# The last bank of the MLP in column halves, and three one-column products on ScalarE

## The chip, the cores and the metric

The kernel runs on one core of one Trainium2 chip. The metric is device time in microseconds (us) of one execution, as a median of several. PE is TensorE, PEld its weight loads, DVE is VectorE, ACT is ScalarE, POOL is GpSimd and SP is SyncE, which here does nothing but issue DMAs in order. L699 means line 699 of the kernel. Lines are given for the kernel before; from line 1415 on the changed kernel's lines stand 3 higher.

## What is computed

Two layers over a sequence of 2048 rows of 512 columns, each a linear attention block and a gated MLP, both added to the row they read:

```python
def _A_ref(x, wqkv, wo):            # H = 32 heads of 16
    q, k, v = ...                   # x @ wqkv, split by head
    phi = lambda t: jnp.where(t > 0, t + 1, jnp.exp(t)) + 1e-6
    pq, pk = phi(q), phi(k)
    kv = jnp.einsum("bhsd,bhse->bhde", pk, v)
    z = jnp.einsum("bhsd->bhd", pk)
    num = jnp.einsum("bhqd,bhde->bhqe", pq, kv)
    den = jnp.einsum("bhqd,bhd->bhq", pq, z)[..., None] + 1e-6
    ...
    return heads_joined(num / den) @ wo

def _B_ref(x, w1, w3, w2):          # w1, w3: 512x1792, w2: 1792x512
    return (_silu(x @ w1) * (x @ w3)) @ w2

x = A_x
x = x + _A_ref(_layernorm(x), A_wqkv, A_wo)
x = x + _B_ref(_layernorm(x), B_w1, B_w3, B_w2)
x = x + _A_ref(_layernorm(x), A_wqkv, A_wo)
x = x + _B_ref(_layernorm(x), B_w1, B_w3, B_w2)
```

## The kernel before

Rows live in SBUF as 16 tiles of 128 rows in fp32 (`x_sb`). Every matrix is scaled by a power of two and split into a high and a low fp16 part, and every product is made of three fp16 passes (`PASSES`). The scale factors are columns of 128x1 in one small tile, `scalars`: each factor is made once and used through the program. Among them are `co` (what the attention's output is multiplied by as it is added to a row, L667 and L668) and `cb` (the same for the MLP's output, L698 to L700). `co` is a product of two factors and `cb` of three; the three multiplications, L668, L699 and L700, are each a 128x1 tensor_tensor on DVE.

In layer 0 the weights of the MLP are prepared while the attention runs: `prepare_w2` (L695) makes the scale of w2 and then `cb`; `w13_group` (L544) takes sums and differences of blocks of w1 and w3 on POOL (L568 to L574) and splits them into high and low parts, the high part on ACT (L440), the low part, `split_late`, on DVE (L442). The order of the instructions on each engine is fixed by the order in which the program issues them: `in_order` pins it in this stage, and tables (FILLS, HOOKS, TURN and others) say where each piece of preparation stands between the pieces of the attention and the MLP. A scheduler places what is not pinned.

The end of layer 0's attention overlaps the start of its MLP. The last row tiles go through `weigh_in`, `weigh_out` (the queries' features, L881 and L1191, the denominator, L1193 to L1212, the low part on POOL, L1220, and a transposing DMA), `attn_out` (matmuls into a bank po) and `attn_add` (L1235 on DVE adds to the row, L1239 and L1240 on ACT take mean and squares). At the same time `mlp_rows` normalises the rows of the next 512 on ACT (L495), makes sums of column blocks (L1263 to L1266, 128x256 each, DVE for half of them) and copies to fp16 on ACT (L1270) and POOL or DVE (L1276).

The MLP works on chunks c of 512 rows and groups g of hidden columns, with seven products of 2x2 blocks in place of eight (`mlp_group`, L1311: matmuls at L518 into the banks ba, bb and bc, copied out by ACT at L1334 and added up by DVE at L1337). The 7 groups are taken in two sets per layer (`SETS`), each over all 4 chunks: 8 passes a layer. The multiplication by w2 goes into banks po, for the first and the second half (`sub`) of each row tile pair. A pass marked "plain" uses `mlp_out_plain` (L1390) with two banks of 128x512, one for each of two row tiles; the last pass of layer 1 is such a pass. Each bank's two column halves are filled by matmuls of their own, 128x256 (L1401).

At the very end (L1593 to L1604) the last group's matmuls are issued bank by bank (`by_bank`), for `sub` 0 and then for `sub` 1: 12 matmuls for the first bank, then 12 for the second. Then `mlp_add` (L1413) adds each bank to its rows in one 128x512 DVE instruction (L1417) and, for `sub` 1, where `engine is None`, stores each row tile by a DMA of 256 KB (`store_row`, L1410) right behind its add. The kernel ends when the last of these stores has landed.

Of the kernel before, what the change touches and what calls it, by code (L numbers as in the profile page):

```python
# [11 lines left out]
AF = mybir.ActivationFunctionType  # L12
OP = mybir.AluOpType
# [5 lines left out]
S, D, F, H = 2048, 512, 1792, 32  # L19
# [69 lines left out]
def kernel(  # L89
# [10 lines left out]
    nc = tc.nc  # L100
    x_rows = x_in.rearrange("b (t p) d -> p (b t) d", p=P)
    out_rows = out.rearrange("b (t p) d -> p (b t) d", p=P)
# [228 lines left out]
    x_sb = view(AT_X, F32, NT, D)  # L331
# [320 lines left out]
    def prepare_vo():  # L652
        yield AT["v"]
        yield from attn_bound("v", 2)
        yield AT["o"]
        yield from attn_bound("o", 3)
        pair_ = [weight_scale(n, info[n], 2.0**14) for n in "vo"]
        for a, _ in zip(*pair_):
            yield a
        for n, i, dst in (("v", 2, wv_s), ("o", 3, wo_s)):  # L660
            for k in range(NK):
                split_late(dst[:, 0, k, :], dst[:, 1, k, :], st_att[i][:, k, :], info[n][2])
                yield heavy[0]
        settle()
        nc.sync.dma_start(att_d["v"], wv_s)
        nc.sync.dma_start(att_d["o"], wo_s)
        co = scaled(info["v"][1], 2.0**-15)  # L667
        nc.vector.tensor_tensor(co, co, info["o"][1], OP.mult)  # L668
        info["co"] = co
        for _ in range(4):  # L670
            w2_load()
# [23 lines left out]
    def prepare_w2():  # L695
        yield has("w2_bound")
        yield from weight_scale("w2", bounds["w2"], 2.0**12)
        cb = scaled(info["w1"][1], 2.0**-5)  # L698
        nc.vector.tensor_tensor(cb, cb, info["w3"][1], OP.mult)  # L699
        nc.vector.tensor_tensor(cb, cb, info["w2"][1], OP.mult)  # L700
        info["cb"] = cb

    AT = {
# [686 lines left out]
    def mlp_out_plain(sub, g, hs, acc, ends, by_bank=False):  # L1390

        cs = slice(sub * P, (sub + 1) * P)
        w2 = w2_s[g]
        order = [(a, bs, n) for a, bs in ((0, (0, 1)), (1, (0,))) for n in range(2)]
        if by_bank:
            order.sort(key=lambda part: part[2])
        for a, bs, n in order:
            for i, qx in enumerate(((0, 3), (2, 1))[n]):
                for b in bs:
                    for half in range(2):  # L1400
                        nc.tensor.matmul(  # L1401
                            acc[n][:, half * HALF : (half + 1) * HALF],
                            hs[:, a, qx, cs],
                            w2_a21[g][:, b] if (i, half) == (0, 1) else w2[:, b, i + half],
                            start=g == ends[0] and i + a + b + half == 0,
                            stop=g == ends[1] and i == 1 and a == 1 and half == 1,
                            skip_group_check=True,
                        )

    def store_row(t):  # L1410
        nc.sync.dma_start(out_rows[:, t, :], x_sb[:, t, :])

    def mlp_add(sub, c, acc, engine):  # L1413

        if len(acc) == 2:
            for t, po in zip((4 * c + sub, 4 * c + 2 + sub), acc):
                nc.vector.scalar_tensor_tensor(  # L1417
                    x_sb[:, t, :], po, info["cb"], x_sb[:, t, :], OP.mult, OP.add
                )
                if engine is None:  # L1420
                    store_row(t)
            return
        a0, a1, a2, a3 = acc
        cb = info["cb"]
        u = view(AT_UV if engine is not None else late_at, F32, 3, HALF)
        x0 = x_sb[:, 4 * c + sub, :].rearrange("p (h n) -> p h n", h=2)
        x1 = x_sb[:, 4 * c + 2 + sub, :].rearrange("p (h n) -> p h n", h=2)

        def add(dst, src, to):
            nc.vector.scalar_tensor_tensor(dst, src, cb, to, OP.mult, OP.add)  # L1430

        nc.scalar.activation(u[:, 0], a0[:, :HALF], AF.Copy, scale=cb)
        if engine is None:

            add(u[:, 1], a0[:, HALF:], u[:, 0])
            add(u[:, 2], a1[:, :HALF], u[:, 1])
            add(x1[:, 0], a1[:, HALF:], x1[:, 0])
            nc.vector.tensor_tensor(x1, x1, u[:, 1:], OP.add)
            nc.vector.tensor_tensor(x0, x0, u[:, 0::2], OP.add)
            add(x0, a2.rearrange("p (h n) -> p h n", h=2), x0)  # L1440
            store_row(4 * c + sub)
            add(x1, a3[:, None, :HALF].to_broadcast([P, 2, HALF]), x1)
            store_row(4 * c + 2 + sub)
            return
        add(x0, a2.rearrange("p (h n) -> p h n", h=2), x0)
        add(x1, a3[:, None, :HALF].to_broadcast([P, 2, HALF]), x1)
        add(x1[:, 0], a1[:, HALF:], x1[:, 0])
        add(u[:, 1], a0[:, HALF:], u[:, 0])
        add(u[:, 2], a1[:, :HALF], u[:, 1])
        engine.tensor_tensor(x0, x0, u[:, 0::2], OP.add)  # L1450
        engine.tensor_tensor(x1, x1, u[:, 1:], OP.add)
# [292 lines left out]
```

## Time and profile before

| | |
|---|---|
| three runs | 1180.77, 1183.33, 1184.78 us; median 1183.33 us |
| the profiled execution | 1182.41 us, with a span of 1180.7 us from first to last instruction |
| PE busy | 1148.0 us, 97% of the span |
| DVE, ACT, POOL busy | 70%, 54%, 36% |
| granted TensorE clock, mean | 0.999 of full speed |

The profile is that of one execution. An instruction's busy time is read with its count; a busy PE is not PE at its peak. "idle before <-X" behind a row is the time in which its engine had nothing to do, and the work that ended it.

### The profile page before, as it was taken

To read this page: it belongs to the slowest core of one execution; us is meant where nothing else is said; L and a number is where in the kernel's file an instruction comes from. 1 tells how busy PE (TensorE), PEld (TensorE's weight loads), DVE (VectorE), ACT (ScalarE), POOL (GpSimd) and SP (SyncE) were. 2 spreads that over 40 slices of the span, in tenths; PEclk is the share of its full clock that TensorE was granted. 3 is DMA by queue.
4 is the path that set the end of the run, shared out by engine and by line. 5 is a ranking of instruction groups with operands and counts; after the bars stand their busy time and mean duration, and the time that the engine had idled before them with its cause. 6 is when DMAs were issued, how large, how long until landed. Compare 5 with 4: busy or idle time off the path is not lost.

```text
span 1180.7 us, 21818 instructions
## 1 busy us (share of the span) xinstructions
PE 1148.0 (97%) x8868; PEld 863.3 (73%) x8868; DVE 831.0 (70%) x1383; ACT 638.8 (54%) x1078; POOL 420.6 (36%) x488
## 2 busy tenths in 40 slices
PE   8999998899999999999999999999999999999998
PEld 3444444788888888888864454467888888888887
DVE  6778898977877886767774559756855775756543
ACT  5777687856544454434456644775544344443422
POOL 5342589402000144235268714684542210102010
PEclk9999999999999999999999999999999999999999
DMA  8977575979542221111416434664351350121000
GB/s 258 342 207 245 113 171 110 270 246 294 159 143 99 81 81 64 63 64 64 81 53 180 103 110 105 130 156 112 99 139 64 126 188 26 57 79 37 1 37 37
DMA packets 163396, 147.43 MB, mean 125 GB/s; under 512 B 129632, under 2 KB 138976, under 8 KB 158688
## 3 DMA queue, kind: packets, MB, share of 16 engines
q1 hardware_dynamic: 163296, 146.04, 42.7%
q8 instruction: 69, 1.13, 0.4%
q14 instruction: 31, 0.25, 0.1%
HBM read 72.48 MB, written 42.07 MB: 97 GB/s over the span
## 4 chain that ended last, share of the span: by engine, by line
PE 60%; DVE 15%; ACT 7%; POOL 6%; DMA 6%; issue 3%; SPq 1%; POOLq 0%; ACTq 0%; DVEq 0%
PE bb L518 16%; PE po L1381 13%; PE bc L518 8%; PE gt L518 5%; PE pk L518 5%; PE ba L518 4%; PE po L518 3%; PE pq L518 3%; DMA arena<-arena 3%; DMA arena<-in_B_w_dram 3%; PE po L1401 2%; DVE arena L1290 2%; DVE arena L1337 2%; DVE arena L442 2%; DVE arena L1430 2%
## 5 line engine op out<-in xcount | busy, mean ns | idle before, releaser
L518 PEld LDWEIGHTS <-arena 128*128 128x128 f16 x6360 | 618.3, 98 | 257.0 <-issue 16.1
L518 PE MATMUL bb<-arena 128*128 128x256 f16 x2688 | 329.5, 273 | 6.6 <-ACT arena L1334 4.0
L1381 PE MATMUL po<-arena 128*128 128x256 f16 x1932 | 234.6, 273 | 9.0 <-ACT arena L1293 6.4
L1381 PEld LDWEIGHTS <-arena 128*128 128x128 f16 x1932 | 187.8, 98 | 35.5 <-ACT arena L1293 9.3
L1295 DVE TENSOR_TENSOR arena<-arena 128x512 f16<-128x512 f32 (+1 forms) x104 | 114.5, 1100 | 105.5 <-ACT arena L1293 105.2
L1334 ACT ACTIVATE arena<-bb 128x512 f32<-128x512 f32 x196 | 114.8, 589 | 122.8 <-PE bb L518 82.1
L518 PE MATMUL bc<-arena 128*128 128x256 f16 x1344 | 165.8, 273 | 0.7 <-ACT arena L1334 0.5
L1293 ACT ACTIVATE arena<-arena 128x512 f16<-128x512 f32 x112 | 99.8, 891 | 120.4 <-DVE arena L1308 46.9
L1289 ACT ACTIVATE arena<-arena,scalars 128x512 f32<-128x512 f32 x112 | 74.7, 667 | 116.0 <-DVE arena L1337 115.5
L1290 DVE SCALAR_TENSOR_TENSOR arena<-arena,scalars 128x512 f32<-128x512 f32 x112 | 88.5, 790 | 51.7 <-ACT arena L1289 51.6
L1337 DVE TENSOR_TENSOR arena<-arena,bc 128x512 f32<-128x512 f32 x112 | 76.5, 683 | 55.0 <-ACT arena L1334 44.4
L1450 POOL TENSOR_TENSOR arena<-arena 128x512 f32<-128x512 f32 x25 | 35.2, 1409 | 207.6 <-DVE arena L1430 207.6
L1430 DVE SCALAR_TENSOR_TENSOR arena<-po,scalars,arena 128x256 f32<-128x256 f32 (+1 forms) x170 | 92.1, 585 | 9.1 <-PE po L1381 7.6
L518 PE MATMUL pk<-arena 128*128 128x512 f16 x384 | 89.8, 384 | 2.2 <-DMA arena<-arena 2.1
L518 PE MATMUL po<-arena 128*128 128x512 f16 x384 | 87.8, 379 | 3.2 <-DMA arena<-arena 2.1
L518 PE MATMUL gt<-arena 128*128 128x512 f16 x384 | 87.8, 379 | 0.6 <-ACT arena L946 0.4
L518 PE MATMUL pq<-arena 128*128 128x512 f16 x384 | 87.6, 379 | 0.1
L518 PE MATMUL ba<-arena 128*128 128x256 f16 x672 | 87.1, 273 | 0.0
L1305 POOL TENSOR_TENSOR arena<-arena 128x256 f32<-128x256 f32 x15 | 11.9, 792 | 148.7 <-DVE arena L1290 148.7
L495 ACT ACTIVATE arena<-arena,nb_all,rs_all 128x512 f32<-128x512 f32 x64 | 50.5, 807 | 26.5 <-POOL nb_all L492 26.3
L1401 PE MATMUL po<-arena 128*128 128x256 f16 x480 | 56.8, 273 | 0.4 <-ACT arena L1293 0.4
L1276 POOL TENSOR_TENSOR arena<-arena 128x512 f16<-128x512 f32 (+2 forms) x33 | 47.4, 1460 | 26.0 <-DMA arena<-arena 19.8
(163 smaller groups left out, 1289.4 us busy)
## 6 DMA issues: line engine op xcount, KB each, us to landing
arena<-xb_d SPq DMA_DIRECT2D x12, 1792.0 KB, 7.1
xb_d<-arena SPq DMA_DIRECT2D x8, 1792.0 KB, 5.9
xt_d<-arena SPq DMA_DIRECT2D x32, 256.0 KB, 2.9
arena<-xt_d SPq DMA_DIRECT2D x32, 256.0 KB, 3.3
arena<-in_B_w_dram SPq DMA_DIRECT2D x8, 896.0 KB, 6.7
arena<-in_B_w_dram SPq DMA_DIRECT2D x28, 256.0 KB, 3.4
w_d<-arena SPq DMA_DIRECT2D x4, 1792.0 KB, 10.8
arena<-w_d SPq DMA_DIRECT2D x4, 1792.0 KB, 6.7
```

The lines of the kernel that those rows point to most:

```text
L495: nc.scalar.activation(dst, x_sb[:, t, :], AF.Identity, scale=rs_all[:, t : t + 1], bias=nb_all[:, t : t + 1],)
L518: nc.tensor.matmul(dst, lhs(a, k), rhs(b, k), start=first and k == 0 and i == 0, stop=last and k == n - 1 and i == len(PASSES) - 1, skip_g ...
L1276: engine_of("rowlow", 2 * c + j).tensor_tensor(nat[:, 1, lo:hi, :], s, nat[:, 0, lo:hi, :], OP.subtract)
L1289: nc.scalar.activation(t, gate, AF.Silu, scale=info["u1"])
L1290: nc.vector.scalar_tensor_tensor(t, up, info["hid"], t, OP.mult, OP.mult)
L1293: nc.scalar.activation(hs[:, 0, lo:hi], t[:, lo:hi], AF.Copy)
L1295: engine.tensor_tensor(hs[:, 1, lo:hi], t[:, lo:hi], hs[:, 0, lo:hi], OP.subtract)
L1334: nc.scalar.activation(dst, bank_, AF.Copy)
L1337: nc.vector.tensor_tensor(dst, dst, bank_, OP.add)
L1381: nc.tensor.matmul(po[:, i * HALF : (i + 1) * HALF], hs[:, a, qx, cs], w2[:, b, qw, :], start=g == ends[0] and i + a + b == 0, stop=g == e ...
L1401: nc.tensor.matmul(acc[n][:, half * HALF : (half + 1) * HALF], hs[:, a, qx, cs], w2_a21[g][:, b] if (i, half) == (0, 1) else w2[:, b, i + ...
L1430: nc.vector.scalar_tensor_tensor(dst, src, cb, to, OP.mult, OP.add)
```

## The change

Two independent edits. The three products of scale factors are issued as an ACT activation Copy with a 128x1 scale, in place of a DVE tensor_tensor. And in the last, plain pass the matmuls of the second bank are ordered by column half (six for columns 0 to 255, then six for 256 to 511), its add is two instructions of 128x256, and its store two DMAs of 128 KB.

```diff
-        nc.vector.tensor_tensor(co, co, info["o"][1], OP.mult)
+        nc.scalar.activation(co, co, AF.Copy, scale=info["o"][1])
...
-        nc.vector.tensor_tensor(cb, cb, info["w3"][1], OP.mult)
-        nc.vector.tensor_tensor(cb, cb, info["w2"][1], OP.mult)
+        nc.scalar.activation(cb, cb, AF.Copy, scale=info["w3"][1])
+        nc.scalar.activation(cb, cb, AF.Copy, scale=info["w2"][1])
...
-        order = [(a, bs, n) for a, bs in ((0, (0, 1)), (1, (0,))) for n in range(2)]
+        order = [(a, bs, n, (0, 1)) for a, bs in ((0, (0, 1)), (1, (0,))) for n in range(2)]
         if by_bank:
-            order.sort(key=lambda part: part[2])
-        for a, bs, n in order:
+            order = [(a, bs, n, h) for n, h in ((0, (0, 1)), (1, (0,)), (1, (1,))) for a, bs, m, _ in order if m == n]
+        for a, bs, n, halves in order:
             for i, qx in enumerate(((0, 3), (2, 1))[n]):
                 for b in bs:
-                    for half in range(2):
+                    for half in halves:
...
             for t, po in zip((4 * c + sub, 4 * c + 2 + sub), acc):
-                nc.vector.scalar_tensor_tensor(
-                    x_sb[:, t, :], po, info["cb"], x_sb[:, t, :], OP.mult, OP.add
-                )
-                if engine is None:
-                    store_row(t)
+                parts = 2 if engine is None and po is acc[1] else 1
+                for i in range(parts):
+                    cols = slice(i * D // parts, (i + 1) * D // parts)
+                    nc.vector.scalar_tensor_tensor(
+                        x_sb[:, t, cols], po[:, cols], info["cb"], x_sb[:, t, cols], OP.mult, OP.add
+                    )
+                    if engine is None:
+                        nc.sync.dma_start(out_rows[:, t, cols], x_sb[:, t, cols])
```

Where the instructions then stand. On DVE at the end of layer 0's attention, where `cb` is made (the piece of the difference around it; scalars is the tile of the factors, pq a PSUM bank with the queries' features, den the denominators, and everything in arena lies in SBUF):

```order
 L403 TENSOR_SCALAR scalars<-scalars 128x1
-L699 TENSOR_TENSOR scalars<-scalars 128x1
+L881 SCALAR_TENSOR_TENSOR pq<-arena,pq 128x512
 L1263 TENSOR_TENSOR arena<-arena 128x256
 L1265 TENSOR_TENSOR arena<-arena 128x256
-L700 TENSOR_TENSOR scalars<-scalars 128x1
-L881 SCALAR_TENSOR_TENSOR pq<-arena,pq 128x512
+L1191 SCALAR_TENSOR_TENSOR pq<-pq,arena 128x512
 L1264 TENSOR_TENSOR arena<-arena 128x256
-L1191 SCALAR_TENSOR_TENSOR pq<-pq,arena 128x512
+L1193 TENSOR_REDUCE den<-pq 128x32
 L1266 TENSOR_TENSOR arena<-arena 128x256
-L1193 TENSOR_REDUCE den<-pq 128x32
```

The two products are gone from DVE, and L881, L1191 and L1193 each stand one or two places earlier among the four column sums. On ACT in the same place the difference is this:

```order
 L1239 ACTIVATE nm_all<-total 128x1
 L1240 ACTIVATE arena,sq_all<-arena,nm_all 128x512
-L1270 ACTIVATE arena<-arena 128x1024
+L699 ACTIVATE scalars<-scalars 128x1
+L700 ACTIVATE scalars<-scalars 128x1
 L1195 ACTIVATE den<-den,scalars 128x32
+L1270 ACTIVATE arena<-arena 128x1024
 L1334 ACTIVATE arena<-bb 128x512
```

The two products are added, and L1195 has moved ahead of the copy L1270. No table load of ACT is added (4 in the built program before, 4 after). L668 has moved from DVE to ACT likewise, some 100 us earlier. On PE no row differs by name (the halves of a bank have one name), on POOL none at all. At the very end the changed kernel has this on DVE (po_12606 and po_12607 are the two banks of the last pass; PE_49 is the semaphore that PE counts up):

```order
L1420 SCALAR_TENSOR_TENSOR arena<-po_12606,scalars,arena 128x512 [waits PE_49]
L1420 SCALAR_TENSOR_TENSOR arena<-po_12607,scalars,arena 128x256 [waits PE_49]
L1420 SCALAR_TENSOR_TENSOR arena<-po_12607,scalars,arena 128x256
L1743 UNCONDITIONAL_BRANCH
```

The last 128x512 add has become two of 128x256; the first of them waits for PE, the second for nothing but its turn. On SP the last store has become two in the same way, each with its own wait for DVE:

```order
L1424 DMA out_dram<-arena 128x512 [waits DMAHW4_49,DVE_49]
L1424 DMA out_dram<-arena 128x256 [waits DMAHW5_49,DVE_49]
L1424 DMA out_dram<-arena 128x256 [waits DMAHW6_49,DVE_49]
```

One DMA more is issued in all; nothing else on SP has moved.

## Rows read from the trace of the kernel before

**Rows 1.** The page: span and the engines' busy time.
```profile
span 1180.7 us, 21818 instructions
PE 1148.0 (97%) x8868; PEld 863.3 (73%) x8868; DVE 831.0 (70%) x1383; ACT 638.8 (54%) x1078; POOL 420.6 (36%) x488
```

**Rows 2.** Timeline of DVE, 186 to 212 us: start, duration, engine, line, what.
```profile
194.52 1.22 DVE L699 TENSOR_TENSOR scalars<-scalars 128x1 f32<-128x1 f32 x1
195.66 0.41 DVE L1263 TENSOR_TENSOR arena<-arena 128x256 f32<-128x256 f32 x1
196.00 0.41 DVE L1265 TENSOR_TENSOR arena<-arena 128x256 f32<-128x256 f32 x1
196.33 1.22 DVE L700 TENSOR_TENSOR scalars<-scalars 128x1 f32<-128x1 f32 x1
197.47 0.68 DVE L881 SCALAR_TENSOR_TENSOR pq<-arena,pq 128x512 f32<-128x512 f32 x1
198.07 0.85 DVE L1264 TENSOR_TENSOR arena<-arena 128x256 f32<-128x256 f32 x1
198.85 0.69 DVE L1191 SCALAR_TENSOR_TENSOR pq<-pq,arena 128x512 f32<-128x512 f32 x1
199.45 0.41 DVE L1266 TENSOR_TENSOR arena<-arena 128x256 f32<-128x256 f32 x1
...
206.23 1.70 DVE L442 SCALAR_TENSOR_TENSOR arena<-arena,scalars 128x512 f16<-128x512 f32 x1 [2.63 <-ACT arena L440]
...
209.31 0.74 DVE L442 SCALAR_TENSOR_TENSOR arena<-arena,scalars 128x512 f16<-128x512 f32 x1
209.97 0.74 DVE L1235 SCALAR_TENSOR_TENSOR arena<-po,scalars,arena 128x512 f32<-128x512 f32 x1
```

**Rows 3.** One line's instructions, the first product, L668.
```profile
L668 DVE TENSOR_TENSOR scalars<-scalars x1: 160/160/160, 89.1 to 89.1; 128x1 f32<-128x1 f32 x1
```

**Rows 4.** Timeline of POOL, 186 to 212 us.
```profile
194.45 1.27 POOL L568 TENSOR_TENSOR arena<-arena 128x512 f32<-128x512 f32 x1
...
196.21 1.32 POOL L570 TENSOR_TENSOR arena<-arena 128x512 f32<-128x512 f32 x1
197.50 1.15 POOL L1220 TENSOR_TENSOR arena<-arena 128x512 f16<-128x512 f32 x1
...
206.11 1.27 POOL L574 TENSOR_TENSOR arena<-arena 128x512 f32<-128x512 f32 x1
```

**Rows 5.** Timeline of PE, 186 to 240 us: the matmuls that waited.
```profile
208.14 1.47 PE L518 MATMUL bb<-arena 128*128 128x256 f16 x12 [1.01 <-ACT arena L1334]
210.78 2.75 PE L518 MATMUL po<-arena 128*128 128x512 f16 x12 [1.16 <-DVE arena L1235]
```

**Rows 6.** Timeline of ACT, 186 to 212 us.
```profile
199.95 1.06 ACT L1270 ACTIVATE arena<-arena 128x1024 f16<-128x1024 f32 x1 [4.30 <-DVE arena L1266]
...
207.51 0.58 ACT L1334 ACTIVATE arena<-bb 128x512 f32<-128x512 f32 x1
207.99 1.32 ACT L440 ACTIVATE arena<-arena,scalars 128x512 f16<-128x512 f32 x2
```

**Rows 7.** Groups of instructions of ACT: an activation of one column.
```profile
L1239 ACT ACTIVATE nm_all<-total 128x1 f32<-128x1 f32 x32 | 6.3, 197 | 18.5 <-DVE arena L1235 18.4
```

**Rows 8.** Timeline, 1172 to 1181 us, the end of the kernel.
```profile
1171.80 5.08 PE L1401 MATMUL po<-arena 128*128 128x256 f16 x45
...
1174.09 3.93 SPq L1411 DMA_DIRECT2D out_dram<-arena  x4
...
1176.91 0.75 DVE L1417 SCALAR_TENSOR_TENSOR arena<-po,scalars,arena 128x512 f32<-128x512 f32 x1 [0.56 <-PE po L1401]
```

**Rows 9.** Timeline, 1140 to 1183 us: two adds of 128x256 from a bank.
```profile
1140.38 0.87 DVE L1430 SCALAR_TENSOR_TENSOR arena<-po,scalars,arena 128x256 f32<-128x256 f32 x2
```

**Rows 10.** DMA issues: line, count, KB each, median us from issue to landing.
```profile
out_dram<-arena SPq DMA_DIRECT2D x16, 256.0 KB, 2.0
...
a_d<-arena SPq DMA_DIRECT2D x4, 128.0 KB, 3.7
```

## The prediction, before the changed kernel was run

> **What bounds the kernel now.** I read the page first, then the timelines of the two places that the change touches. The page says that PE is busy for 1148.0 of 1180.7 us [rows 1]: all idle time of PE together is 32.7 us, and a change can gain only where PE waits, or behind its last matmul. So two questions remain. Does PE wait for anything that the three products hold up? And how long is the end, from the last matmul to the landing of the last store?
>
> The end first. The last matmuls stop at 1176.88 (1171.80 + 5.08), the last add starts at 1176.91 and takes 0.75, the last of four issues on SP ends at 1178.02 (1174.09 + 3.93), and the span ends at 1180.7 [rows 1, 8]. These 3.8 us are serial: add, issue, landing. The add cannot be cut to nothing and the landing is a DMA's own time, so what an overlap could take out is part of the 0.75.
>
> The products next. L668 took 0.16 us [rows 3]. L699 and L700, the same operation on one column, took 1.22 each [rows 2]. They end at 195.74 and 197.55, and POOL's L568 and L570 end at 195.72 and 197.53 [rows 4]: each product waited for the POOL instruction that was running. The column sum L1264 took 0.85 where its equals took 0.41, beside POOL's L1220, and L442 took 1.70 where another took 0.74, beside L574 [rows 2, 4]. All of these DVE instructions read two operands from SBUF. L881 and L1191, with one operand in a PSUM bank, kept to 0.68 and 0.69 though POOL was running [rows 2, 4].
>
> **The change part by part.**
>
> *L668 to ACT.* DVE is relieved of 0.16 us [rows 3], and ACT gets a one-column activation of 0.197 [rows 7]. Between -0.16, if DVE were on the path there, and +0.2, if ACT were, I take 0.
>
> *L699 and L700 to ACT.* On ACT they add 0.4 us (twice 0.197, rows 7) in a stretch in which ACT sat idle for 4.30 us before L1270 [rows 6]; that hides them. On DVE, from the start of each product to the start of the next instruction, 1.14 us are freed twice (194.52 to 195.66 and 196.33 to 197.47, rows 2): 2.28 us. But much of this is not DVE's to keep, since the port that the products waited for is what the next instruction waits for too:
>
> - L881 now starts at about 194.5 and takes 0.6 to the next start. L1263 stands behind it at 195.1, reads two operands from SBUF, and finds L568 running: it starts at 195.66 as before. The first 1.14 us have only covered L881.
> - L1265 at 196.0, as before. L1191 runs at 196.35 beside L570. L1264 stands ready at 196.95 and waits for L570 to end. L700 in the same position got in between L570 and L1220, so I let L1264 do so: 197.5 to 197.9.
> - With that, L1220 on POOL starts some 0.38 later than 197.50. L1193, as wide as L1191, is given the 0.6 from L1191's start to the next, and L1266 at 198.5 waits for the later L1220: about 199.05 to 199.45, against 199.45 to 199.86 before. Of 2.28 us, 0.4 are left here.
>
> Who waits for this? PE waits 1.01 us at 208.14 for ACT's copy L1334 and 1.16 us at 210.78 for DVE's L1235 [rows 5]. L1235 stands behind the second L442, at 209.31, that one waits for the second L440 of the pair at 207.99 on ACT, and this pair needs the last block difference of POOL, L574, which ends at 207.38 [rows 2, 4, 6]. POOL's twelve instructions from L568 to L574 follow each other nearly without a gap (the first and the last stand in rows 4), so L574 sets the earliest time of the pair: 207.99 - 207.38 = 0.61 us earlier at the most. With POOL pushed back once by 0.38, 0.23 is left. I take 0.2 us of gain and keep both ends: 2.28 us, if all that DVE is freed of reached PE, and a loss (the slow rival below).
>
> The rule beside these rows is in the Trainium skill, SBUF — State Buffer, section "SBUF: two separate sides": GpSimd and VectorE share one pair of ports as an exclusive lock, taken also by a VectorE instruction with two SBUF inputs, and the loser waits out the whole instruction. The trace agrees for L699, L700, L1264 and the long L442; it is hard on an edit that counts 2.28 us as freed. Without the rule the sum here would be the 2.28; with it, the 0.2.
>
> *The last bank in halves.* The wish is that the first half's add runs beside the last six matmuls. The built order says otherwise: of the two adds only the first waits for PE, and the second waits for nothing. A second add that may follow with no wait of its own is right only if the first one's wait already covers the matmuls of both halves. So both adds start behind the last matmul, and the order of the matmuls inside the bank is worth nothing: same count, same shape. Two 128x256 adds back to back took 0.87 [rows 9], one of 128x512 takes 0.75 [rows 8]: +0.12 us. The first store is issued while the second add runs. The last store, issued 0.12 later, is half as large. Its landing lies between 1.0 (half of the 2.0 of a 256 KB store) and 3.7 (the 128 KB stores to a_d, beside other traffic) [rows 10]. I take 2.0, since the quiet end of the kernel is where the 2.0 was measured; the ends of the range are -1.0 and +1.7.
>
> The Trainium skill, PSUM — Partial Sum Buffer, section "PSUM bank collisions raise a hardware error", has the reason: two engines must not touch one bank in the same partitions at one time, disjoint columns included, so the tools put a dependency between them. By the rule the split costs the 0.12; without it the first add would be over before the last matmul, and only the second add would lie behind it.
>
> **The sum**, against the profiled execution's own 1182.41 us (span 1180.7 and 1.71 around it): 0 for L668, -0.2 for L699 and L700, +0.12 for the end: 1182.3. The median of the runs shown is 1183.33, 0.92 above the profiled one; the forecast for a median is therefore 1183.33 - 0.1 = **1183.2 us**. About 0.3%, or 3.5 us, is what a measurement of this kernel can tell from no change: the three runs alone span 4.0 us.
>
> **The rivals.**
>
> 1. *The halves do overlap.* Then the end has one add of 0.44 (half of the 0.87, rows 9) in place of 0.75: -0.31, with the -0.2 above a gain of 0.5: 1182.8. For it speaks only the diff; the missing second wait speaks against it.
> 2. *All of DVE's 2.28 us reach PE.* That needs POOL off the path: 1183.33 - 2.28 + 0.12 = 1181.2. For it: PE's two waits at 208 to 211 us sum to 2.17. Against it: L574's end.
> 3. *Slower: POOL loses the port.* Place: POOL between L570 and L574. Each DVE instruction that now gets in ahead of a POOL one pushes all of POOL back, and ACT's L440, DVE's L442 and PE's po matmuls behind it. Price: three column sums of 0.41 and the L442 at 206.23, which comes earlier and may get ahead of L574, with 0.74: 1.97 us, less the slack of 0.61: 1.36, and 0.12 at the end: 1184.8. It decides from a push of 0.61 on, that is from the second instruction that gets ahead. For it: the queue order now puts the sums closer together. Against it: in the rows of before POOL loses little (L570 took 1.32 against 1.27).
>
> **How the numbers follow.** Forecast 0.62, rival 1 0.05, rival 2 0.13, rival 3 0.20. No case leaves the 3.5 us by itself; what can is the scatter of the runs, 2.6 below and 1.45 above their median, on top of rival 2 or 3. That gives 0.06 for faster, 0.90 for the same, 0.04 for slower. The range goes from 1180.0 (rival 2 less part of the scatter, or a short last landing) to 1186.0 (rival 3 and the scatter above, or a long last landing).
>
> **What would show it.** In the profile after: L699 and L700 on ACT near 0.2 each behind L1240; on DVE L1263 still starting when L568 ends; L1220 on POOL a few tenths later; PE's waits for L1334 and L1235 shorter by tenths, not by 2 us. At the end both half adds behind the last matmul, the first at once, the second about 0.4 later, and the last store's issue 0.1 later. A first half add that starts before the last matmul ends, a PE without the two waits at 208 and 211 us, or L574 ending after 208 us would prove the forecast's steps wrong; a time outside 1180.0 to 1186.0 would prove the whole reading wrong.

## The result, and the profile after

Over 20 runs each, the median was 1184.09 us with the change (1181.21 to 1189.35) and 1181.91 without it (1180.77 to 1184.90). The ratio is 1.0020, with a 95% interval of 1.0012 to 1.0029: slower by 0.2%. The forecast was no measurable change, 1183.2 us; its base was the median of three runs, 1183.33, which lies 1.4 us above that of the twenty.

The median hides the form of the loss. The changed kernel's runs are spread unevenly: 11 of them lie between 1181.21 and 1184.73, as those of before do (1180.77 to 1184.90), and 9 between 1185.32 and 1189.35, where none of the 20 of before lies. So the change does not cost 2 us in every execution. It makes a part of the executions 3 to 7 us longer. The profiled execution of the changed kernel, 1189.35 us, is one of these, and its page says so at once: PE is busy for 3.6 us more than before [rows 1] with the same number of matmuls.

```profile
span 1187.6 us, 21822 instructions
...
PE 1151.6 (97%) x8868; PEld 864.6 (73%) x8868; DVE 830.8 (70%) x1381; ACT 638.8 (54%) x1081; POOL 420.7 (35%) x488
```

More busy time for equal work means slower matmuls. The timeline of PE in the changed kernel shows where (start, duration, engine, line, what, and in brackets the idle time before the row and what ended it):

```profile
207.99 1.47 PE L518 MATMUL bb<-arena 128*128 128x256 f16 x12
211.71 4.10 PE L518 MATMUL po<-arena 128*128 128x512 f16 x12 [2.26 <-DVE arena L1235]
215.61 2.50 PE L518 MATMUL bb<-arena 128*128 128x256 f16 x18
...
236.84 2.72 PE L518 MATMUL bb<-arena 128*128 128x256 f16 x12 [3.67 <-ACT arena L1334]
239.36 1.92 PE L518 MATMUL bc<-arena 128*128 128x256 f16 x12
```

Before, these 12 matmuls into po took 2.75 us [rows 5]; the other rows of PE that answer to them, and one that is needed below, were these in the kernel before:

```profile
199.58 1.25 PE L518 MATMUL bb<-arena 128*128 128x256 f16 x10 [2.07 <-DMA arena<-arena]
...
213.36 2.13 PE L518 MATMUL bb<-arena 128*128 128x256 f16 x18
...
232.15 1.47 PE L518 MATMUL bb<-arena 128*128 128x256 f16 x12 [1.59 <-ACT arena L1334]
233.45 1.47 PE L518 MATMUL bc<-arena 128*128 128x256 f16 x12
```

So po took 1.35 us more and the 18 matmuls behind it 0.37: 1.72 us. The same happens 25 us later, with 1.25 and 0.45: 1.70 us. The windows of the changed kernel give the reason (stretch; its length; busy time and count of PE, PEld, DVE, ACT, POOL; then the granted clock of PE, the share of the DMA engines, GB/s):

```profile
213.00:217.00 4.00, 4.00 (x17) 2.03 (x16) 3.20 (x7) 2.52 (x7) 0.00 (x0) 0.58 0.92 268
217.00:236.00 19.00, 16.18 (x149) 14.35 (x147) 16.41 (x24) 13.25 (x23) 10.18 (x11) 1.00 0.82 194
236.00:240.00 4.00, 3.15 (x16) 2.16 (x15) 3.61 (x7) 2.90 (x6) 0.00 (x0) 0.61 1.00 390
```

The granted clock falls to the lower of its two levels (1.2 in place of 2.4 GHz) behind a wait of 2.26 us, comes back, and falls again behind one of 3.67 us. In the kernel before it is 1.00 all through this stage:

```profile
205.00:245.00 40.00, 35.85 (x303) 29.42 (x302) 34.97 (x60) 31.36 (x59) 14.60 (x15) 1.00 0.82 240
```

Where do these two waits come from? Before, PE waited twice near 210 us, 1.01 us for ACT's copy L1334 and 1.16 us for DVE's L1235, with 12 matmuls between [rows 5]. Now the first of the two waits is gone, and the second is as long as both were. The rows of ACT show why:

```profile
196.53 0.28 ACT L699 ACTIVATE scalars<-scalars 128x1 f32<-128x1 f32 x1
196.85 0.30 ACT L700 ACTIVATE scalars<-scalars 128x1 f32<-128x1 f32 x1
...
202.37 0.62 ACT L430 ACTIVATE arena<-arena 128x512 f16<-128x512 f32 x1
...
207.36 0.57 ACT L1334 ACTIVATE arena<-bb 128x512 f32<-128x512 f32 x1
208.94 1.33 ACT L440 ACTIVATE arena<-arena,scalars 128x512 f16<-128x512 f32 x2 [1.01 <-POOL arena L574]
...
234.15 0.51 ACT L440 ACTIVATE arena<-arena,scalars 128x256 f16<-128x256 f32 x1 [4.07 <-DMA arena<-in_B_w_dram]
```

This execution as a whole runs 0.98 us later from 80 us on (a difference of the start, told of below). Against that, L1334 is 1.13 us earlier than before (207.36 - 0.98 = 206.38, before 207.51 [rows 6]), so the 12 matmuls into bb have no wait. It is earlier because it stands at the end of an unbroken row of ACT instructions that begins with L430, and L430 no longer waits for DVE's L1212. In the kernel before it did:

```profile
202.37 0.63 ACT L430 ACTIVATE arena<-arena 128x512 f16<-128x512 f32 x1 [0.66 <-DVE arena L1212]
```

The pair L440 behind L1334 is no earlier (207.96, before 207.99): it waits 1.01 us for POOL's L574. So L1235, which stands behind this pair, is where it was. All that the change gave to PE was the same idle time in one piece.

The second wait follows from the first loss. Behind 217 us the transposing DMAs on SP come later by 2.6 and then 3.9 us (the second stands behind DVE's three L1276, which took 3.75 us beside POOL, before 3.23), and behind them on SP the loads of raw weights. ACT's L440 at 234.15 waits 4.07 us for one of these loads. In the kernel before it had no wait there:

```profile
229.14 0.51 ACT L440 ACTIVATE arena<-arena,scalars 128x256 f16<-128x256 f32 x1
```

PE's wait for the L1334 behind it grows from 1.59 to 3.67 us.

These terms add up to most of the 6.9 us by which the span is longer, measured as the lag of PE's matmuls behind those of before: 1.0 us from the start, 1.6 over the merged wait and the first fall, 2.1 for the longer wait at 236 us, and 1.1 of the second fall, the rest of which went into waits that PE had behind it before. Another 1.0 us came at 286 us, where PE waited 0.15 us in the profile of before:

```profile
286.31 1.47 PE L518 MATMUL bb<-arena 128*128 128x256 f16 x12 [1.15 <-DVE arena L1337]
```

What is left are pieces of under 0.4 us.

DVE and POOL in the same stretch, first DVE:

```profile
195.38 0.69 DVE L881 SCALAR_TENSOR_TENSOR pq<-arena,pq 128x512 f32<-128x512 f32 x1
195.97 1.01 DVE L1263 TENSOR_TENSOR arena<-arena 128x256 f32<-128x256 f32 x1
196.91 0.41 DVE L1265 TENSOR_TENSOR arena<-arena 128x256 f32<-128x256 f32 x1
197.24 0.69 DVE L1191 SCALAR_TENSOR_TENSOR pq<-pq,arena 128x512 f32<-128x512 f32 x1
197.84 0.88 DVE L1264 TENSOR_TENSOR arena<-arena 128x256 f32<-128x256 f32 x1
198.65 0.68 DVE L1193 TENSOR_REDUCE den<-pq 128x32 f32<-128x512 f32 x1
199.25 0.77 DVE L1266 TENSOR_TENSOR arena<-arena 128x256 f32<-128x256 f32 x1
...
200.32 0.69 DVE L1212 TENSOR_TENSOR arena<-pq,den 128x512 f32<-128x512 f32 x1
...
206.08 1.71 DVE L442 SCALAR_TENSOR_TENSOR arena<-arena,scalars 128x512 f16<-128x512 f32 x1 [2.35 <-ACT arena L440]
...
210.91 0.74 DVE L1235 SCALAR_TENSOR_TENSOR arena<-po,scalars,arena 128x512 f32<-128x512 f32 x1
```

and POOL:

```profile
195.43 1.28 POOL L568 TENSOR_TENSOR arena<-arena 128x512 f32<-128x512 f32 x1
...
198.41 1.33 POOL L1220 TENSOR_TENSOR arena<-arena 128x512 f16<-128x512 f32 x1
...
207.19 1.72 POOL L574 TENSOR_TENSOR arena<-arena 128x512 f32<-128x512 f32 x1
```

The denominators' chain took the whole gain: L1193 and L1212 stand at 197.67 and 199.34 without the 0.98, 2.1 and 2.3 us earlier than in the profile of before:

```profile
199.78 0.68 DVE L1193 TENSOR_REDUCE den<-pq 128x32 f32<-128x512 f32 x1
...
201.64 0.69 DVE L1212 TENSOR_TENSOR arena<-pq,den 128x512 f32<-128x512 f32 x1
```

The column sums gained less (L1266 ended 0.8 us earlier), and what hangs on POOL gained nothing. L1263 now carries the wait for L568 that L699 carried before (1.01 us, its equal L1265 0.41), L1264 and L1266 wait in the same way, and L442, which before came behind L574, now gets in ahead of it: L574 takes 1.72 us in place of 1.27 [rows 4]. L1235 starts at 210.91, or 209.93 without the 0.98; before it was 209.97 [rows 2]. So of the 2.28 us that the products held on DVE, all arrived at L1212; 1.13 of it arrived at L1334 and took away PE's first wait, and 0.04 arrived at L1235, which ends the second.

Last, the end of the changed kernel:

```profile
1182.74 0.75 DVE L1420 SCALAR_TENSOR_TENSOR arena<-po,scalars,arena 128x512 f32<-128x512 f32 x1 [0.34 <-PE po L1401]
1183.52 1.85 SPq L1424 DMA_DIRECT2D out_dram<-arena  x3
1184.05 0.88 DVE L1420 SCALAR_TENSOR_TENSOR arena<-po,scalars,arena 128x256 f32<-128x256 f32 x2 [0.56 <-PE po L1401]
```

Both half adds stand behind the last matmul, 0.88 us for the two against 0.75 for the one [rows 8].

### The profile page after: what moved, and what is told of

Read it like the earlier page. It is cut to its first block, busy times and chain, and to the rows that moved or that the text cites. A ratio compares the mean times of both kernels' runs of the same rounds, so it can differ in the third digit from the quotient of the medians.

```text
span 1187.6 us, 21822 instructions
## 1 busy us (share of the span) xinstructions
PE 1151.6 (97%) x8868; PEld 864.6 (73%) x8868; DVE 830.8 (70%) x1381; ACT 638.8 (54%) x1081; POOL 420.7 (35%) x488
## 3 DMA queue, kind: packets, MB, share of 16 engines
q8 instruction: 69, 1.13, 0.4%
## 4 chain that ended last, share of the span: by engine, by line
PE 61%; DVE 17%; ACT 6%; DMA 6%; POOL 5%; issue 3%; SPq 1%; DVEq 0%; POOLq 0%; ACTq 0%
PE bb L518 16%; PE po L1381 12%; PE bc L518 8%; PE po L518 5%; PE pk L518 5%; PE gt L518 5%; PE pq L518 4%; PE ba L518 3%; DMA arena<-arena 3%; PE po L1401 2%; DVE arena L1290 2%; DMA arena<-in_B_w_dram 2%; DVE arena L1433 2%; DVE arena L1337 2%; DVE arena L1295 2%
## 5 line engine op out<-in xcount | busy, mean ns | idle before, releaser
L1334 ACT ACTIVATE arena<-bb 128x512 f32<-128x512 f32 x196 | 114.7, 589 | 125.9 <-PE bb L518 84.9
L442 DVE SCALAR_TENSOR_TENSOR arena<-arena,scalars 128x512 f16<-128x512 f32 (+2 forms) x60 | 49.1, 834 | 11.0 <-ACT arena L440 9.9
```

The lines of the kernel that those rows point to most:

```text
L442: lambda: nc.vector.scalar_tensor_tensor(lo, src, scale, hi, OP.mult, OP.subtract)
L1334: nc.scalar.activation(dst, bank_, AF.Copy)
```

## The experiments

The theory at this point: the move to ACT gave nothing, but it made PE's two short waits into one of 1.8 to 2.3 us, and behind a wait of that length the granted clock falls in a part of the executions. Rivals: the halves; the extra ACT work as such; chance of the first measurement.

Each kernel of an experiment was timed in five rounds beside the kernel before. The table gathers them; the ratio is taken against the runs of before in the same batch and is not the quotient of two medians. "Wait" is PE's idle time near 210 us in the kernel's profile, "long" the number of runs above 1185 us, a bound set after the first measurement was known. The runs of before come to 132 with those of all batches; their medians differ from batch to batch, 1181.16 to 1182.44.

| kernel | wait, us | median, us | ratio, 95% interval | long |
|---|---|---|---|---|
| before | 1.01 and 1.16 | 1181.16 to 1182.44 | | 1 of 132 |
| changed, first | 2.26 | 1184.09 | 1.0020, 1.0012 to 1.0029 | 9 of 20 |
| changed, again (e5) | 2.15 | 1183.61 | 1.0011, 1.0002 to 1.0021 | 3 of 11 |
| changed, third (e12) | 2.03 | 1182.46 | 1.0007, 0.9996 to 1.0018 | 1 of 11 |
| e1, products only | 1.84 | 1182.02 | 1.0013, 1.0000 to 1.0027 | 3 of 11 |
| e7, two products | 2.22 | 1183.15 | 1.0005, 0.9996 to 1.0015 | 1 of 12 |
| e9, products, less work | 2.68 | 1182.63 | 1.0007, 0.9994 to 1.0020 | 1 of 12 |
| e3, products, wait filled | none | 1182.51 | 1.0013, 1.0004 to 1.0022 | 0 of 11 |
| e6, products, sum moved | 1.06 | 1181.29 | 0.9998, 0.9989 to 1.0006 | 0 of 11 |
| e11, changed, sum moved | 1.06 | 1181.13 | 0.9998, 0.9989 to 1.0008 | 0 of 11 |
| e2, halves only | 0.75 and 1.16 | 1181.08 | 0.9999, 0.9989 to 1.0008 | 0 of 11 |
| e4, before, filled | 0.89 and 0.30 | 1181.86 | 1.0001, 0.9992 to 1.0010 | 0 of 11 |
| e8, before, sum moved | 0.72 and 0.96 | 1183.17 | 0.9999, 0.9990 to 1.0008 | 0 of 11 |
| e10, before, less work | 0.77 and 1.83 | 1181.88 | 0.9996, 0.9986 to 1.0006 | 0 of 11 |

### One part alone: e1 and e2

e1 has only the three products on ACT, e2 only the last bank in halves (their diffs are the two parts of the change's own).

> Only the three products on ScalarE; the end of the kernel as before. The clock theory: in the changed kernel PE's two waits near 208 us (1.01 and 1.16 us) have become one of 2.26 us in front of the po matmuls, the granted clock falls to half behind it, and those twelve matmuls take 4.1 in place of 2.75 us; so this kernel has the same one long wait, runs between 1181 and 1189 us like the changed kernel, and its median lies some 2 us above the kernel before. The theory of the end (two adds and two stores cost the time): median as before, 1182 us.

> Only the last bank in column halves; the products on VectorE as before. The clock theory: the time of the kernel before plus 0.1 us, 1182.0 us median, no run near 1187 us more often than before. The theory of the end: the 2 us of the changed kernel, 1184 us.

e1 was slower, 1.0013 with an interval that begins at 1.0000, with 3 of 11 runs at 1185.53 to 1188.11. e2 was as before, 0.9999, none long. So in these two the long runs come with the products and not with the halves. e1's own profile is of a short run (1183.02 us): PE's waits have become one there too, but the 12 matmuls behind it keep their 2.75 us.

```profile
210.88 2.75 PE L518 MATMUL po<-arena 128*128 128x512 f16 x12 [1.84 <-DVE arena L1235]
```

The end can be measured by itself from the profiles of both sorts, as the time from the last matmul's end to the end of the span. With the last bank whole it is 3.78 to 3.80 us in nine profiles; with halves it is 3.62 to 3.64 in five. The halves save 0.16 us. The page of the changed kernel says how:

```profile
out_dram<-arena SPq DMA_DIRECT2D x15, 256.0 KB, 2.0
...
out_dram<-arena SPq DMA_DIRECT2D x2, 128.0 KB, 1.7
```

A store of 128 KB landed 0.3 us sooner than one of 256 KB, and that outweighs the 0.13 us of the longer add.

### The wait filled: e3 and e4

Behind P7, the 12 matmuls into bb, PE gets some matmuls of 128x512 on ones into a bank that nothing reads: seven in e3 (which has the products on ACT), four in e4 (the kernel before).

```diff
+            if name == "P7" and layer == 0 and state["groups"] == 0:
+                with in_order("PE"):
+                    steps_[name]()
+                    hold = acc_bank("hold")
+                    for _ in range(7):
+                        nc.tensor.matmul(hold..., ones16, ..., start=True, stop=True)
+                continue
...
-                attn_add(NT - AFTER + i, attn_out(NT - AFTER + i))
+                with in_order(*(("PE",) if i == 1 else ("none",))):
+                    po = attn_out(NT - AFTER + i)
+                attn_add(NT - AFTER + i, po)
```

> The three products on ScalarE, and in front of the po matmuls of the last row tile seven matmuls of 128x512 on ones into a bank that nothing reads (about 1.5 us of PE time, no other engine's order changed), so that PE works through most of its 2.26 us wait. The clock theory: no fall of the granted clock behind it, the po matmuls in 2.75 us, no runs at 1185 to 1189, median 1181.5 us. The theory that VectorE takes the shared port from POOL at this place: the filling changes nothing there, POOL's L574 and VectorE's L1235 as late as in the changed kernel, median 1184 us.

> The kernel before with four such matmuls in the same place, where it waits 1.16 us. The clock theory: the waits of the kernel before are short enough as they are in most runs, so the median stays within 0.5 us of 1181.9; if its own runs near 1184.8 us are the same fall of the clock, they become rarer. The port theory: no change at all.

e4 was as before. e3 lost the long runs (its highest is 1184.42), but not the higher median, 1182.51 with a ratio of 1.0013: a miss for half of the theory. Its profile (1182.22 us) shows PE without the wait at 210 us, and, behind 190 us, two falls of the clock at other places:

```profile
197.84 2.00 PE L518 MATMUL bb<-arena 128*128 128x256 f16 x10 [2.08 <-DMA arena<-arena]
199.64 2.21 PE L518 MATMUL ba<-arena 128*128 128x256 f16 x10
...
208.21 1.67 PE L1372 MATMUL hold<-ones 128*128 128x512 f16 x7
209.72 2.75 PE L518 MATMUL po<-arena 128*128 128x512 f16 x12
...
231.58 2.06 PE L518 MATMUL bb<-arena 128*128 128x256 f16 x12 [2.08 <-ACT arena L1334]
```

The 10 matmuls into bb at 198 us took 1.25 us in the profile of before, behind a wait of 2.07 us; here they take 2.00 behind 2.08: a wait of one length, once with and once without a fall. Most of what was lost there went into PE's later wait. The fall at 231 us, behind 2.08 us where before had 1.59, was not taken up. Seven of e3's 11 runs have a mean granted clock of 0.997 or less, so falls at such places may be what keeps its median up; only this one profile shows where they were.

### The wait shortened by real work: e6 and e8

From L568 to L574 POOL's instructions follow each other nearly without a gap. The first block sum of the second group, L568, is given to DVE; PE's order is untouched. e6 has this with the products on ACT, e8 with the kernel before.

```diff
-        engine_of("w13", g).tensor_tensor(a22, a21, a22, OP.add)
+        (nc.vector if g == 1 else engine_of("w13", g)).tensor_tensor(a22, a21, a22, OP.add)
```

> The three products on ScalarE, the last bank whole as before, and the first block sum of the second group (L568 at 194.6 us) moved from POOL to VectorE; PE's order is untouched. It takes 1.27 us out of POOL's unbroken chain that ends in L574. Theory: ACT's L440 pair, which waits 0.61 us for L574 in the products-only run, starts right behind L1334, so PE's one wait for L1235 shrinks from 1.84 to 1.2 or 1.3 us; the clock stays full in every run, no run of 11 is above 1184.5 us, and the median is 0.5 us under the kernel before, about 1180.7. Rival (the long runs belong to the products on ScalarE whatever PE waits): 3 or 4 of 11 above 1184.5 us, median 1182. Rival (the port: the sum on VectorE waits out POOL's L1276 and holds up VectorE's own chain): L574 earlier by 1.2 but PE's wait still 1.8 or more, median 1182.

> The kernel before with L568 of the second group on VectorE in place of POOL, nothing else. Theory: L574 ends 1.2 us earlier; PE's wait for L1334 keeps its 1.0 us, since ACT has other work before it, and the one for L1235 falls from 1.16 to about 0.55; no run above 1184.5, median 0.5 us below the kernel before. Rival (PE has slack later, so that a gain at 210 us is given back): the waits shrink as said and the ratio is 1.000 within 0.0005. Rival (port): VectorE loses more than POOL gains, both waits as before or longer, ratio over 1.000.

In e6 the wait shrank to 1.06 us and no run was long, as the theory said; on the same chip in the same batch, the unedited change had 3 of 11. The gain of 0.5 us in the median wasn't resolved (0.9998, interval 0.9989 to 1.0006). In e8 both waits shrank a little (to 0.72 and 0.96, the second expected at 0.55), a wait of 0.72 us that before did not have came up at 202.77, and nothing was gained in all: 0.9999, as the rival with slack further on said. In both kernels the edit also shortened PE's wait at 198 us (1.46 and 1.38 us, where before had 2.07). That wait cannot make the long runs by itself, since the kernel before has it and had 1 long run of 132.

### Again, and two products: e5 and e7

> The changed kernel once more, unedited, for a second profile and more runs. Theory (PE's two waits near 210 us became one, and in a part of the executions the granted clock falls behind it): 4 to 6 of 11 runs above 1184.5 us, the rest between 1180.5 and 1184; in the profile a single PE wait of 1.8 to 2.3 us for DVE's L1235, and no wait for ACT's L1334 before it. In a long profiled run the clock near 214 us is 0.5 to 0.7; in a short one it is 1.00. Rival (the long runs of the first measurement were a chance of that hour or chip): at most 1 of 11 above 1184.5.

e5 gave 3 of 11 long runs, ratio 1.0011: the slowdown is there again and is smaller. Its long runs end at 1185.74, not far above the highest of before in the same batch, 1184.93. Its profile is of a run of 1185.18 us, and it speaks against too simple a story: a wait of 2.15 us, no fall of the clock behind it or later while PE had work, and yet a long run. Its time went in small pieces, of which the second row shows the largest:

```profile
211.09 2.75 PE L518 MATMUL po<-arena 128*128 128x512 f16 x12 [2.15 <-DVE arena L1235]
...
280.68 1.47 PE L518 MATMUL bb<-arena 128*128 128x256 f16 x12 [0.82 <-DVE arena L1337]
```

The second is the place where the profile of before waited 0.15 us and the first one of the changed kernel 1.15. Between 225 and 440 us e5's run lost 2.6 us in this way. So the bound of 1185 us doesn't sort the runs by the clock alone.

e7 has only L699 and L700 on ACT.

> Only the two products L699 and L700 on ScalarE, L668 on VectorE and the last bank whole as before. Theory: these two alone bring ACT's copy L1334 forward, so it behaves as all three did: PE's wait for L1334 gone, one wait of 1.8 to 2.3 us for L1235, 2 to 5 of 11 runs above 1184.5 us, ratio 1.000 to 1.003. Rival (L668, 80 us earlier, has a part): both PE waits stay at 1.0 and 1.2 us, none above 1184.5, ratio 1.000.

The one wait was there, 2.22 us, with full clock behind it, and 1 of 12 runs was long (1187.02). The waits came out as the theory said, the number of long runs between the theory and its rival: it doesn't settle whether L668 has a part.

### A longer wait: e9 and e10

Six of P7's 12 matmuls are left out, so the wait for L1235 is 0.65 us longer while every other engine keeps its order. e9 has the products on ACT, e10 is the kernel before.

```diff
             for w in range(2):
+                if w and wx is P7 and layer == 0 and state["groups"] == 0:
+                    continue
```

> The three products on ScalarE, the last bank whole as before, and 6 of the 12 matmuls of the first group's product P7 left out (the half of its bank w = 1, so a part of the hidden layer lacks one of seven block products); no other engine's order differs. These 6 matmuls run just ahead of PE's one wait for L1235 and take 0.65 us, so the wait grows from 1.8 to 2.2 us to 2.5 to 2.9 us with L1235 itself unmoved. Theory (the granted clock falls behind one long wait, the more often the longer it is): more of the runs are long than of the kernel with all matmuls: 6 or more of 11 above 1184.5 us, median 1184 to 1187, although PE has less to do; in a long profiled run the clock near 214 us is 0.5 to 0.7. Rival (the length of that wait has no part in it): 2 to 4 of 11 above 1184.5 us, median 1182 to 1183.

> The kernel before with the same 6 matmuls of P7 left out, nothing else; the three products stay on VectorE. PE's two waits stay two, 1.0 us for L1334 and 1.16 + 0.65 = 1.8 us for L1235, with 6 matmuls of 0.8 us between them. Theory, if the length and nearness of PE's waits decide: now the kernel before, too, has long runs, 2 to 5 of 11 above 1184.5 us. Rival (the ScalarE products as such make the long runs): none of 11 above 1184.5 us and the ratio 1.000. If two waits with work between them are harmless while one of 1.8 us is not, it is also none; then the fill between is what counts, as in the filled run.

Here the theory failed in its number. In e9 the wait was 2.68 us, the longest of all at this place, and the clock stayed full in the profile:

```profile
211.19 2.75 PE L518 MATMUL po<-arena 128*128 128x512 f16 x12 [2.68 <-DVE arena L1235]
```

One run of 12 was long (1188.18, mean clock 0.995), two by the bound of 1184.5 us in the expectation, not six: the rival's number. e10 kept two waits, 0.77 and 1.83 us with six matmuls between, and had no long run. So a longer wait doesn't make long runs more frequent in any way that 12 runs show. (Six of P7's matmuls are missing in both kernels, so neither computes the whole layer.)

### The whole change with the sum moved, and the change a third time: e11 and e12

> The whole change (three products on ScalarE, last bank in halves) and, beside it, the block sum L568 of the second group on VectorE in place of POOL. Theory (a single PE wait of 2.0 us or more puts the clock at risk, a shorter one does not, and the long runs come from there): PE's one wait for L1235 is 1.0 to 1.3 us, no run of 11 above 1185 us, median within 0.6 us of the kernel before. Rival (the halves, or the ScalarE products whatever PE waits, make the long runs): 3 to 5 of 11 above 1185 us.

> The changed kernel a third time, on the chip and in the hour of the repaired one. Theory: PE's wait for L1235 is 1.8 to 2.3 us again; 2 to 5 of 11 runs above 1185 us, and those with a mean clock of 0.998 or less; median 0.5 to 2 us above the kernel before. Rival (the first measurement's long runs were of that chip): at most 1 of 11 above 1185.

e11 came out as expected: a wait of 1.06 us, highest run 1183.19, 0.9998 of before. Here too the wait at 198 us was shorter, 1.85 us. e12 had its median 1.3 us above before, as expected, but only 1 of 11 long (1186.41, mean clock 0.997): the rival's number, and the ratio's interval, 0.9996 to 1.0018, includes 1. With 3 of 11 in e5, 1 of 11 here and 9 of 20 at first, the share of long runs is not a constant of the kernel, and why the first measurement had most is open.

e11 also shows why a gain of 1.2 us at 210 us does not appear at the end. PE in e11:

```profile
210.04 2.75 PE L518 MATMUL po<-arena 128*128 128x512 f16 x12 [1.06 <-DVE arena L1235]
...
630.37 2.32 PE L518 MATMUL gt<-arena 128*128 128x512 f16 x10 [1.07 <-DVE arena L961]
```

At 630 us PE now waits 1.07 us for L961 of DVE, where the profile of before had no such wait. That L961 took 1.66 us (0.77 in e1's profile), because POOL's L1137 had begun just ahead of it. DVE and POOL in e11:

```profile
628.66 1.66 DVE L961 SCALAR_TENSOR_TENSOR arena<-arena,scalars 128x512 f16<-128x512 f32 x1 [2.32 <-POOL arena L432]
```

```profile
628.62 1.15 POOL L1137 TENSOR_TENSOR arena<-arena 128x512 f16<-128x512 f32 x1
```

The same wait, 1.07 us, stands in the profiles of e6 and e7; these are single profiles, so how often it comes is open.

## Why the prediction was wrong, point by point

**The failed step: who waits for this.** The prediction found both of PE's waits and followed L1235 back to L574. Of L1334 it only gave the wait, and it treated the two as idle time to be summed, of which some tenths might go. On DVE it followed the column sums only and found that 0.4 of the 2.28 us were left at L1266. It gave the other two between them, L1191 and L1193, their new times, but did not ask who waits for them: through L1195 and L1212 they lead to ACT's L430 and on to L1334, and 2.3 us arrived at L1212 on DVE and 1.13 at the copy. That is the mechanism of the second rival, for one of the two waits. With that wait gone and the end of the other fixed, the two become one, of 1.84 to 2.26 us in the profiles with all of P7. One of the forecast's own signs, a PE without both waits at 208 and 211 us, came half true, and another came true as written: L574 ended at 208.91, behind 208 us (207.93 without the 0.98). And it had no rival in which idle time of PE is worth more in one piece than in two. The trace of before held the row for one, which the prediction didn't read:

```profile
44.72 4.45 PE L518 MATMUL pk<-arena 128*128 128x512 f16 x12 [2.08 <-DMA arena<-arena]
```

These are 12 matmuls of the form that takes 2.75 us at 210 [rows 5]; behind a wait of 2.08 us they took 4.45. This one row would have given a rival with a place and a price: 1.7 us for one fall.

**How far that is shown.** Shown: the falls and their price in one profile of the changed kernel (1.72 and 1.70 us, and 2.08 us of longer wait between them); that the one wait comes with the products and not with the halves (e1, e2); and that without it no run was long (e3, e6, e11: none of 33). Kernels with the one wait had 18 long runs of 77, or 9 of 57 without the measurement that suggested the bound; those with the products on DVE had 1 of 176. All six kernels' ratios with the one wait lie at 1.0005 or above, those of the other kernels but e3 at 1.0001 or below. The mean granted clock of each run points the same way. A profile without a fall ahead of the last matmul has 1.000 (e2, e6), one with a single fall 0.999 or 0.998, and one with three 0.996 (the changed kernel, e3). Of the runs with the one wait, none of the 38 at 0.999 or 1.000 was long, 16 of the 28 at 0.997 or less were, and all eight at 0.996 or less. So most long runs had more falls than the others.

Not shown: that these falls stood behind the one wait. The mean doesn't tell the place, and of the 156 runs with the products on DVE that have it recorded, 33 lie at 0.997 or less and all but one of these are short. Two profiles of long runs were taken; the first has the fall at 210 us, e5's has none there. Not shown either is what decides in which execution the clock falls. The length of the wait alone doesn't (e9). And e3 stays slower by 0.13% without the wait and without a long run.

**L668.** DVE was relieved of 0.16 us, and ACT got 0.282, not 0.197; no experiment sees it, as said.

**L699 and L700.** On ACT they took 0.28 and 0.30 us, where the row of one column with a constant scale gave 0.197; idle time hides them, as said. On DVE most steps came as written: L1263 waits out L568 and L1264 waits out L570. L1220 was to start 0.38 us later and started 0.07 earlier, and L1266 ended 0.8 us earlier in place of 0.4. The gain of 0.2 us at L1235 was 0.04: L574 did not end earlier but 0.55 later (208.91 - 0.98 = 207.93, before 207.38 [rows 4]). This is the mechanism of the slow rival at the place it named, L442 ahead of L574, with a push of 0.55 us in place of up to 1.97, which the slack of 0.61 took up. By the Trainium skill, SBUF — State Buffer, section "SBUF: two separate sides", the loser of the shared port waits out the whole instruction of the winner; the trace agrees (L574 1.72 us against 1.27, L961 1.66 against 0.77), and e11's row says what follows for any forecast: an edit that moves DVE against POOL by a microsecond can draw new pairs of them, 400 us further on too.

**The last bank in halves.** That the two adds stand together behind the last matmul was right, and so was their price (0.13 us, forecast 0.12). The landing was mis-sized: I took 2.0 us for the 128 KB store as for a 256 KB one, where it took 1.7, and the end as a whole became 0.16 us shorter. It was forecast 0.12 us longer.

**What a measurement can tell.** The 0.3% in the text came from the span of three runs. Twenty runs on each side told 0.2% from nothing, with an interval of 0.17% width. Within its own bound the forecast of no change held, and the time lay inside the range; as a statement on the direction it was wrong. That 1184.09 lies near the slow rival's 1184.8 is luck: that rival had POOL's push beyond its slack make the loss, and here it was the clock and a longer wait.

## What to carry to other kernels

When an edit frees an engine, follow every chain that gets earlier to the engine that bounds the kernel, and draw its waits anew: two short waits with work between them can become one, at the same idle sum. Before pricing idle time of PE by its length, look in the trace for equal matmuls behind a wait that took half as long again; if there are any, a wait of that length can have a second price. And where runs fall into groups, count the groups before reading a median.

## What the runs showed of the hardware that was not expected

Waits of one length are followed by a lower clock in some executions and not in others, at each of three places where PE waits 2.0 us or more. At 44 us, in the kernel with only the halves, the matmuls that took 4.45 us before ran at full clock behind nearly the same wait:

```profile
44.29 2.76 PE L518 MATMUL pk<-arena 128*128 128x512 f16 x12 [2.06 <-DMA arena<-arena]
```

In the 14 profiles, the waits of 2.03 to 2.64 us at this place were followed by the lower clock in 8 of 10. At 198 us it was 1 of 11 (2.02 to 2.48 us), at 210 us 1 of 5 (2.03 to 2.68 us); near 232 us it was both of two (2.08 and 3.67 us). Between 180 and 1160 us no wait under 2 us was followed by a lower clock in any of the 14. Early in the kernel it was otherwise: at 20 us, behind waits of 1.6 to 1.9 and 0.41 us with one matmul between, the lower clock came in 4 of 14 (e3, e4, e7, e12).

The start makes a part of the spread in time that every kernel has. Aligned with the profile of before, the others run from 2.1 us earlier to 1.0 later at 50 us, and keep that to 190 us; the late ones are the eight with the lower clock at 44 us, the early ones the six without (four of these six had it at 20 us). The spans of the six are 1178.8 to 1180.5 us, those of the eight 1180.3 us and more.
